# Loads, copies and tile pools at the start and in the last pair, and fewer filler matmuls, in a kernel of attention, soft MoE and feed-forward

## The chip, the cores and the metric

The kernel runs on one core of one Trainium2 chip. The metric is device time in microseconds (us) of one execution, median of three runs. The engines are TensorE (PE in the rows), VectorE (DVE), ScalarE (ACT), GpSimd (POOL) and SyncE (SP, whose queue issues nearly all DMAs); PEld is TensorE's weight load.

## The reference

Three layers follow each other. Attention works on 2 x 8 heads of 768 tokens and 64 values; a query sees only the keys of its own bucket, and a bucket is made of six sign bits:

```python
q_bits = (np.einsum('bhsd,dk->bhsk', q, proj) > 0)      # likewise k_bits
mask = q_bucket[:, :, :, None] == k_bucket[:, :, None, :]
scores = np.where(mask, scale * np.matmul(q, k.transpose(0, 1, 3, 2)), -1000000000.0)
attn = np.exp(scores - np.max(scores, axis=-1, keepdims=True))
attn = attn / (np.sum(attn, axis=-1, keepdims=True) + 1e-09)
x = np.matmul(attn, v)                                   # then (1536, 512)
# soft MoE: 8 experts, 4 slots each
logits = x @ phi
d = softmax over tokens of logits; slot_input = d.T @ x
slot_out[e] = np.maximum(slot_input[e] @ w1[e], 0.0) @ w2[e]
x = softmax over slots of logits @ slot_out
# feed-forward, 512 -> 2048 -> 512
h = x @ w_in
out = (h - np.tanh(h)) @ w_out
```

The inputs are float32, but w_in and w_out come as 64-bit floats and are converted. w1 and w2 are 17 MB each, w_in and w_out 8 MB each.

## The kernel before

The 16 heads are worked on in eight pairs, numbered 0 to 7. Query and key of a pair come as 128 x 768 tiles `xq` and `xk` (64 rows for each head). Matmuls run with rounded fp32 values: `QA` and `KA` hold the rounded part of a head in rows 0 to 63 and the bucket rows and offsets above, `QB` and `KB` hold a copy of the rounded part and the remainder. For each pair the units are: `m`, one tile of maxima (L447 matmul into `pm`, L449 reduce on VectorE into `mx`); `f`, which makes a row of maxima out of them (L454 `mh`, L457 transpose `pc`, L460 and L461, and a small DMA of `row` into `QA`); `s0` and `s1`, scores and exponential for the first and second head (L508 `pst`, L511 on ScalarE into a tile `e`, L521 sum `es` on GpSimd); `a`, product with v (L532 and L536, `pav`); `xr`, `xe`, `x2`, `x3` (sums `pr`, copy `xtu`, scaling and transposed tokens `px`, `xtok`) and `lg`, the MoE logits (L615 `pl`, L618, L624, L625). `wl` and `wc` load and convert w_in.

Pair 0 has units of its own. `const` issues the constants `ct`, `qk` the loads, `hp` and `h` the rounded halves (L379, L381), `b0` the sign bits: L355 writes 4 x 32 partitions of one PSUM tile `pb` (two quarters for the query, two for the key), L361 turns the products into bits in place, and `rows0` (L369 on ScalarE, L371 on VectorE) makes bucket rows of `QA` and `KA` from them. `kc` copies a half of `KA` into `kh1`, `d` copies into `QB` and `KB`, all by DMA (L166). `keep` and `warm` are matmuls into a tile that nobody reads (L718).

The order is written by hand. `START`, `FIRST`, `STEP`, `STEP2` and `LAST` are lists of unit names: START runs first, FIRST in pair 0, STEP to pair 5, STEP2 in pair 6 and LAST in pair 7; units of the next pair are in the list of the one before. `MOE` and `RUN` order the rest. Each engine works in this order of its own instructions, each waiting for its inputs, and SyncE's queue is in order as well.

Tiles come from pools with as many buffers as a number says; a new use waits for the last reader of the old one. `e` tiles come from two pools of NE1 = 12 and NE2 = 7; the second closes within pair 6, so that pairs 6 and 7 have NE1 tiles. Room that a closed pool leaves is opened as a ring of slots for pieces of the expert weights, 1 MB each (`load_pieces`, L249): `RING` gives how many at each place, 21 in all. The third place is in pair 6, when the wide pools close; the fourth and fifth are in pair 7. After the 21st, a piece waits for the release of the slot that it reuses.

`moe` computes dispatch weights `sT`, and then runs the units of MOE: `F` slot inputs (L957), `R`, `T`, `W` and `X` first and second expert product (L970, L934, L981), `H`, `y` (L998) and `z` (L1007) the last experts, `p` and `d` products with w_in (L1036, L1055); `k` is a `keep_clock` of one matmul (two rows in the trace) into `ph`, never read (L805). The last stage, from 300 us, multiplies with w_out in three passes (L1277 to L1279).

Of the kernel before, what the change touches and what calls it, by code (L numbers as in the profile page):

```python
# [68 lines left out]
START = ("const.0 oi.0 qk.0 hp3.0 warm.4 const.1 const.2 b0.0 wl.0 h1.0 h0.0 hp2.0 wk0a.0 wq0v.0 keep.1 wl.0 m.0 wk1a.0 "  # L69
        "kc.0 m.0 m.0 v.0 m.0 m.0 keep.3 l0.0 keep.3 m.0 keep.1 m.0 wq1a.0 m.0 qk.1 keep.1 h2.1 oi.1 h3.1 m.0 keep.3 "  # L70
        "m.0 wl.0 l1.0 m.0 d.0 m.0 v1.0 keep.1 fa.0 m.0 m.0 m.0 v.1 b0.1 l3.0 m.0 m.0 h0.1 m.0 fb.0 h1.1 wl.0 wc.0 "
        "wk1a.1 wq1a.1 s0.0 l2.0 fz.0 wq0a.1 s0.0 v2.0 kc.1 qk.2 s0.0 wk0v.1 keep.1 oi.2 wc.0 s0.0 a.0 wc.0 s0.0 s0.0").split()
FIRST = ("a a a a a a a wc lp fy g0 g1 m l0 l1 wc lp a wl m a vy g2 s0 h1 l2 h3 h0 v qk s1 s0 m s1 m xe d h2 m s0 m m e "
        "wl s1 m xr wl v1 m s1 m m s0 b lg m s0 m s1 s1 m m s0 e s0 s0 m s1 x2 e m e wl lp s1 lp m s1 x3 f2 lp s0 lp wc "
        "s1 s0").split()
# [1336 lines left out]
```

## Time and profile before

| | us |
|---|---|
| median of 3 runs | 455.56 (454.02 to 455.61) |
| the profiled execution | 454.35 |
| its span | 452.6 |
| TensorE busy in the span | 430.2 (95%) |
| VectorE, ScalarE, GpSimd busy | 323.4, 272.5, 285.5 |

The times below are from the profiled execution; its span starts with the first instruction. A row of the windows view gives the stretch, its length, the busy time of each engine with the number of its instructions, the granted TensorE clock (1.00 is full), the mean busy share of the 16 DMA engines, and GB/s. A row of the timeline gives the start, the time from the first to the last of the instructions grouped there, engine, line, operation, output and inputs, shape, count, and, in brackets, the idle time before it and what ended that.

### The profile page before, as it was taken

The numbers are of one execution on the slowest core, as the hardware profiler recorded it, in microseconds if no ns is written. First come the engines' busy times: TensorE is split into PE (matmuls) and PEld (weight loads), VectorE is DVE, ScalarE is ACT, GpSimd is POOL, SyncE is SP. The second block draws the span as 40 slices with busy tenths as digits, with TensorE's granted clock in tenths as the row PEclk, the third lists the DMA queues.
The fourth block names the chain that finished last, engine by engine and source line by source line (L and its number), as shares of the span: only waits on it lengthen the run. The fifth ranks groups of instructions, "written<-read, shape, count | busy, mean of one in ns | idle before, by whom it ended". The sixth has DMA issues, their size and how long they took to land. (4 is left out here: it accounts for less than half of the span.)

```text
span 452.6 us, 7545 instructions
## 1 busy us (share of the span) xinstructions
PE 430.2 (95%) x2621; PEld 298.6 (66%) x2621; DVE 323.4 (71%) x585; ACT 272.5 (60%) x525; POOL 285.5 (63%) x287
## 2 busy tenths in 40 slices
PE   5868999999999999999999998999999999999994
PEld 2446476685858668566767343667777788888883
DVE  4899999999999887484416458299989975454541
ACT  4496658576676947164630111298898978575751
POOL 8759839789797978979660200047788864535350
PEclk9888999999999999999999999999999999999999
DMA  6736454636254543565859999980000003000004
GB/s 197 184 132 168 99 176 135 190 106 187 72 144 159 149 149 117 221 202 234 314 205 421 419 419 420 416 370 0 2 1 2 0 0 141 0 2 0 1 2 146
DMA packets 18166, 71.33 MB, mean 158 GB/s; under 512 B 3492, under 2 KB 4616, under 8 KB 13000
## 3 DMA queue, kind: packets, MB, share of 16 engines
q1 hardware_dynamic: 17976, 70.75, 44.9%
q8 instruction: 23, 0.38, 0.3%
q14 instruction: 23, 0.19, 0.1%
q10 hardware_dynamic: 144, 0.02, 0.0%
HBM read 60.09 MB, written 3.15 MB: 140 GB/s over the span
## 5 line engine op out<-in xcount | busy, mean ns | idle before, releaser
L521 POOL TENSOR_TENSOR es<-es,e 128x512 f32<-128x512 f32 x73 | 92.9, 1286 | 14.4 <-ACT e L511 13.8
L511 ACT ACTIVATE e<-pst 128x512 f32<-128x512 f32 x144 | 77.7, 596 | 40.3 <-PE pst L508 36.1
L449 DVE TENSOR_REDUCE mx<-pm 128x1 f32<-128x512 f32 x144 | 90.2, 677 | 11.7 <-PE pm L447 11.3
L508 PE MATMUL pst<-QA,KA 128*128 128x256 f32 (+1 forms) x192 | 66.7, 362 | 2.1 <-DVE QB L419 1.1
L536 PE MATMUL pav<-e,tv 128*64 128x512 f32 (+1 forms) x384 | 65.0, 489 | 0.0
L508 PE MATMUL pst<-QB,KB 128*128 128x256 f32 (+1 forms) x192 | 63.4, 344 | 0.0
L1227 DVE SCALAR_TENSOR_TENSOR ph<-win,ph 128x512 f32<-128x512 f32 (+1 forms) x64 | 35.7, 558 | 32.6 <-ACT win L1222 31.3
L447 PE MATMUL pm<-KA,QA 96*128 96x512 f32 x192 | 52.7, 361 | 3.6 <-POOL zrw L303 2.9
L1258 POOL TENSOR_TENSOR split<-win,split 128x512 fp32r<-128x512 f32 x31 | 44.9, 1447 | 14.1 <-ACT split L1253 14.1
L1279 PE MATMUL po<-w,split 128*128 128x512 f32 x128 | 51.0, 398 | 0.0
L1277 PE MATMUL po<-w,split 128*128 128x512 f32 x128 | 50.6, 396 | 0.0
L1278 PE MATMUL po<-w,split 128*128 128x512 f32 x128 | 50.4, 394 | 0.0
L536 PEld LDWEIGHTS pav<-e,tv 128*64 128x64 f32 x384 | 26.3, 137 | 33.6 <-issue 27.3
L521 POOL TENSOR_TENSOR es<-e 128x512 f32<-128x512 f32 x30 | 38.9, 1299 | 14.6 <-PE pr L550 9.8
L1258 POOL TENSOR_TENSOR ghl<-win,ghl 128x256 fp32r<-128x256 f32 x32 | 24.2, 756 | 37.0 <-ACT ghl L1253 37.0
L508 PEld LDWEIGHTS pst<-QA,KA 128*128 128x128 f32 x192 | 37.1, 193 | 12.4 <-ACT e L511 4.6
L1222 ACT ACTIVATE win<-ph 128x512 f32<-128x512 f32 (+1 forms) x64 | 30.8, 482 | 22.7 <-PE ph L1215 22.1
L447 PEld LDWEIGHTS pm<-KA,QA 96*128 96x128 f32 x192 | 32.3, 195 | 15.9 <-DVE mx L449 3.9
L1228 DVE SCALAR_TENSOR_TENSOR win<-win,ph 128x512 f32<-128x512 f32 (+1 forms) x64 | 35.5, 555 | 8.3 <-ACT win L1223 0.2
L1223 ACT ACTIVATE win<-win,ct 128x512 f32<-128x512 f32 (+1 forms) x64 | 39.5, 617 | 2.1
L508 PEld LDWEIGHTS pst<-QB,KB 128*128 128x128 f32 x192 | 37.3, 194 | 3.5
L1279 PEld LDWEIGHTS po<-w,split 128*128 128x128 f32 x128 | 24.0, 188 | 7.7 <-POOL split L1258 2.7
(230 smaller groups left out, 803.1 us busy)
## 6 DMA issues: line engine op xcount, KB each, us to landing
...
```

What stands on the lines that cost most here:

```text
L447: nc.tensor.matmul(pm[:, j * 256:j * 256 + c1 - c0], QA[s][h][:96, c * P:(c + 1) * P], KA[s][h][:96, c0:c1], start=True, stop=True)
L449: nc.vector.reduce_max(m, pm.rearrange("p (c k) -> p c k", c=len(cs)), axis=AX.X)
L508: nc.tensor.matmul(pst[:, j * 256:j * 256 + c1 - c0], K[h][:, c * P:(c + 1) * P], Q[h][:, c0:c1], start=x == 0, stop=x == 1)
L511: nc.scalar.activation(e, pst, AF.Exp, scale=0.125)
L521: eng.tensor_tensor(q[0], y, e, ALU.add)
L536: nc.tensor.matmul(pav[i][k][64 * h:64 * h + 64, :], tv[i][:, h, c, :], e2[h][:, j * 256:j * 256 + c1 - c0], start=False, stop=c == KT - 1 ...
L1223: nc.scalar.activation(w, z, AF.Square, bias=ct[:, C_QA:C_QA + 1])
L1227: nc.vector.scalar_tensor_tensor(self.ph[p], z, Q_C, self.ph[p], ALU.mult, ALU.mult)
L1258: (eng or nc.gpsimd).tensor_tensor(gl[p], g, gh[p].bitcast(F32), ALU.subtract)
L1277: nc.tensor.matmul(po, gh[p][:, us], wo.half(f, 0), start=f == 0, stop=False)
L1278: nc.tensor.matmul(po, gh[p][:, us], wo.half(f, 1), start=False, stop=False)
L1279: nc.tensor.matmul(po, gl[p][:, us], wo.half(f, 0), start=False, stop=f == NF - 1)
```

## The change

At the start, `qk.0` goes ahead of the constants, and `b0` of pair 0 is split into `bq` and `bk`, which each take a PSUM tile and compare 64 partitions. The bucket rows of the query are written by ScalarE, those of the first key half by VectorE. The copies `kh1`, `QB` and `KB` of pair 0 are made by ScalarE from `xk` and `xq` (rounded on writing) instead of DMAs from `KA` and `QA`. The `keep` units stand elsewhere, and pair 1's loads come ahead of w_in's. NE1 and NE2 become 10 and 9. `zrw` and `vzw` move from pool `lap` to a pool `zap`, which `head_x` closes; `lap` is closed by itself, before. `RING` gets one slot more in its third place, and the places of pair 7 become 4, 1, 2 and 1 instead of 4, 3 and 2; 21 stay. LAST is ordered anew. In MOE the eight `k.1` are left out.

```diff
-WIDE, NE1, NE2 = 5, 12, 7
+WIDE, NE1, NE2 = 5, 10, 9
-RING, HOLD = (4, 1, 3, 4, 3, 2, 3, 1), 4
+RING, HOLD = (4, 1, 4, 4, 1, 2, 1, 3, 1), 4
-START = ("const.0 oi.0 qk.0 hp3.0 warm.4 const.1 const.2 b0.0 wl.0 h1.0 h0.0 hp2.0 wk0a.0 wq0v.0 keep.1 wl.0 m.0 wk1a.0 "
+START = ("oi.0 qk.0 const.0 hp3.0 const.1 h1.0 warm.4 const.2 bq.0 bk.0 qk.1 wl.0 h0.0 hp2.0 wq0a.0 wk0v.0 keep.1 l0.0 "
...
-LAST = ("a a a a lp xe a s0 s0 lp a a a s0 lp s0 s1 s1 s1 s0 lp xr s0 a a lp x2 x3 s1 s1 lp s1 s0 s0 s0 lp s1 s1 s1 lg "
+LAST = ("a a a s0 lp s0 a a a s0 a lp a s1 xr s0 s0 s1 xe s1 s1 s1 lp s0 lp s1 a a a a lp s0 lp s1 lp x2 s0 lg s1 s0 s1 "
...
-MOE = ("k.1 k.1 k.1 F.0 F.1 R.1 T.0 R.0 W.0 F.2 X.0 W.1 T.2 k.1 T.1 k.1 wm.2 R.2 H.0 F.3 wm.3 X.1 k.1 T.3 W.2 H.1 X.2 "
+MOE = ("F.0 F.1 R.1 T.0 R.0 W.0 F.2 X.0 W.1 T.2 T.1 wm.2 R.2 H.0 F.3 wm.3 X.1 T.3 W.2 H.1 X.2 y.0.1 y.0.0 z.0.0 wm.0 "
...
-        last_x, head_x, early_x, wide_x, xq_x, mid_x, raw_x = (ExitStack() for _ in range(7))
+        last_x, head_x, lap_x, early_x, wide_x, xq_x, mid_x, raw_x = (ExitStack() for _ in range(8))
-        lap = pool("lap", 1, head_x)
+        zap = pool("zap", 1, head_x)
+        lap = pool("lap", 1, lap_x)
-        zrw = lap.tile([P, KT, P], F32R, name="zrw")
-        vzw = lap.tile([P, P], F32R, name="vzw")
+        zrw = zap.tile([P, KT, P], F32R, name="zrw")
+        vzw = zap.tile([P, P], F32R, name="vzw")
...
-        def bits0(i):
-            pb = bt0[i] = psum("pb")
-            halves(i, pb)
-            nc.vector.tensor_scalar(pb[:, :HALF], pb[:, :HALF], 0.0, None, ALU.is_gt)
+        def bits0(i, which):
+            pb = psum("pb")
+            for x in which:
+                bt0[i, x] = pb
+            halves(i, pb, range(2 * which[0], 2 * which[-1] + 2))
+            b = pb[64 * which[0]:64 * which[-1] + 64, :HALF]
+            nc.vector.tensor_scalar(b, b, 0.0, None, ALU.is_gt)
...
-            copy(kh1[i][64:], KA[i % 3][1][:64])
+            nc.scalar.activation(kh1[i][64:], xks[i][64:], AF.Copy)
...
+        def dup(i, which, h):
+            s, t, r0 = i % 3, i % 2, slice(64 * h, 64 * h + 64)
+            if which == 0:
+                nc.scalar.activation(QB[t][h][64:], xqs[i][r0], AF.Copy)
+            else:
+                nc.scalar.activation(KB[t][h][:64], xks[i][r0], AF.Copy)
...
-                if i == last and half.get((i, 0)) == len(SEQ) and len(slots) == sum(RING[:4]) and not xtu and last in pav:
-                    head_x.close()
+                if i == last and len(slots) == sum(RING[:4]) and not xtu and i - 1 not in tv:
+                    lap_x.close()
                     load_pieces(RING[3])
                     open_ring(RING[4], rctx)
                     load_pieces(RING[4])
-                if i == last and half.get((i, 1)) == len(SEQ) and len(slots) == sum(RING[:5]):
-                    last_x.close()
+                if i == last and half.get((i, 0)) == len(SEQ) and len(slots) == sum(RING[:5]) and last in pav:
+                    head_x.close()
                     open_ring(RING[5], rctx)
                     load_pieces(RING[5])
+                if i == last and half.get((i, 1)) == len(SEQ) and len(slots) == sum(RING[:6]):
+                    last_x.close()
+                    open_ring(RING[6], rctx)
+                    load_pieces(RING[6])
```

What this does to the order of instructions is shown at three places. First VectorE at the start, from the first bits to the first `mh`, before:

```order
L361 TENSOR_SCALAR pb<-pb 128x384
L371 TENSOR_SCALAR QA_131<-pb,ct 24x384 x2
L449 TENSOR_REDUCE mx<-pm 128x1 x2
L449 TENSOR_REDUCE mx<-pm 128x2
L449 TENSOR_REDUCE mx<-pm 128x1 x2
L449 TENSOR_REDUCE mx<-pm 128x2
L449 TENSOR_REDUCE mx<-pm 128x1 x2
L449 TENSOR_REDUCE mx<-pm 128x2
L449 TENSOR_REDUCE mx<-pm 128x1 x2
L449 TENSOR_REDUCE mx<-pm 128x2
L454 TENSOR_REDUCE mh<-mx 128x6
```

and the same stretch in the change:

```order
L366 TENSOR_SCALAR pb<-pb 64x384 x2
L376 TENSOR_SCALAR KA_138<-pb,ct 24x384 x2
L461 TENSOR_REDUCE mx<-pm 128x1 x2
L461 TENSOR_REDUCE mx<-pm 128x2
L461 TENSOR_REDUCE mx<-pm 128x1 x2
L461 TENSOR_REDUCE mx<-pm 128x2
L461 TENSOR_REDUCE mx<-pm 128x1 x2
L461 TENSOR_REDUCE mx<-pm 128x2
L461 TENSOR_REDUCE mx<-pm 128x1 x2
L466 TENSOR_REDUCE mh<-mx 128x6
```

The compare is split in two, VectorE writes the key rows and not the query rows, and `mh` stands behind eleven reduces where it stood behind twelve. ScalarE from the first half on, before:

```order
L381 ACTIVATE QA_131<-xq 64x768
L381 ACTIVATE KA_135<-xk 64x768
L369 ACTIVATE KA_135<-pb,ct 24x384 x4
L369 ACTIVATE QA_131<-pb,ct 24x384 x2
L381 ACTIVATE KA_137<-xk 64x768
L381 ACTIVATE QA_133<-xq 64x768
```

and in the change:

```order
L386 ACTIVATE QA_134<-xq 64x768
L386 ACTIVATE KA_138<-xk 64x768
L374 ACTIVATE QA_134<-pb,ct 24x384 x2
L374 ACTIVATE KA_138<-pb,ct 24x384 x2
L394 ACTIVATE kh_199<-xk 64x768
L374 ACTIVATE QA_134<-pb,ct 24x384 x2
L386 ACTIVATE KA_140<-xk 64x768
L386 ACTIVATE QA_136<-xq 64x768
L412 ACTIVATE KB_145<-xk 64x768
L410 ACTIVATE QB_142<-xq 64x768
L412 ACTIVATE KB_145<-xk 64x768
L410 ACTIVATE QB_142<-xq 64x768
```

Query rows of the first head come first, and five copies stand between them and around pair 1's halves. Second, SyncE's queue in pairs 6 and 7 (`w` is a piece of the expert weights, `row` the maxima of pair 7, `rt` and the like small copies), before:

```order
L249 DMA w<-in_moe_w_dram 128x2048
L166 DMA QB_140<-QA_132 64x768
L166 DMA KB_143<-KA_136 64x768
L166 DMA QB_141<-QA_133 64x768
L166 DMA KB_144<-KA_137 64x768
L249 DMA w<-in_moe_w_dram 128x2048 x3
L166 DMA QA_132<-row 1x6x128
L166 DMA QA_133<-row 1x6x128
L166 DMA zrw<-zrow 1x6x128 x4
L249 DMA w<-in_moe_w_dram 128x2048 x13
```

and in the change:

```order
L250 DMA w<-in_moe_w_dram 128x2048
L167 DMA QB_143<-QA_135 64x768
L167 DMA KB_146<-KA_139 64x768
L167 DMA QB_144<-QA_136 64x768
L167 DMA KB_147<-KA_140 64x768
L250 DMA w<-in_moe_w_dram 128x2048 x4
L167 DMA QA_135<-row 1x6x128
L167 DMA QA_136<-row 1x6x128
L167 DMA zrw<-zrow 1x6x128 x4
L250 DMA w<-in_moe_w_dram 128x2048 x12
```

One piece goes from behind the rows to ahead of them. Third, TensorE at the start of MOE, from `sT`'s filler to the product behind T.1, before:

```order
L805 MATMUL po_3069<-ct 128x256
L805 MATMUL ph_3064<-ct 128x256 x3
L957 MATMUL po_3066<-w,sT 32x512 x16
L957 MATMUL po_3067<-w,sT 32x512 x16
L970 MATMUL po_3068<-ct,hold_3187 128x128 x4
L934 MATMUL po_3069<-ct,hold_3188 128x128 x4
L957 MATMUL po_3066<-w,sT 32x512 x16
L981 MATMUL po_3067<-w,hold_3188 32x512 x16
L934 MATMUL po_3068<-ct,hold_3188 128x128 x4
L970 MATMUL po_3069<-ct,hold_3187 128x128 x4
L805 MATMUL ph_3064<-ct 128x256
L970 MATMUL po_3066<-ct,hold_3187 128x128 x4
```

and in the change:

```order
L822 MATMUL po_3077<-ct 128x256
L974 MATMUL po_3074<-w,sT 32x512 x16
L974 MATMUL po_3075<-w,sT 32x512 x16
L987 MATMUL po_3076<-ct,hold_3192 128x128 x4
L951 MATMUL po_3077<-ct,hold_3193 128x128 x4
L974 MATMUL po_3074<-w,sT 32x512 x16
L998 MATMUL po_3075<-w,hold_3193 32x512 x16
L951 MATMUL po_3076<-ct,hold_3193 128x128 x4
L987 MATMUL po_3077<-ct,hold_3192 128x128 x4
L987 MATMUL po_3074<-ct,hold_3192 128x128 x4
```

The three matmuls ahead of the first L957 and the one between the two L970 are gone, and nothing else has moved; one filler stays ahead, into `po`.

## Rows read from the trace of the kernel before

**Rows 1.** Windows: length, busy us (instructions) by engine, clock, DMA share, GB/s.

```profile
20.00:30.00 10.00, 7.34 (x36) 5.19 (x34) 9.06 (x19) 9.05 (x16) 4.84 (x3) 0.83 0.14 42
60.00:200.00 140.00, 139.78 (x928) 95.62 (x928) 123.15 (x228) 92.33 (x176) 118.20 (x118) 1.00 0.51 156
249.30:264.20 14.90, 14.90 (x137) 4.77 (x136) 4.78 (x9) 1.96 (x4) 2.96 (x12) 1.00 1.01 417
```

**Rows 2.** Timeline of all engines at the start, from the first load.

```profile
0.73 0.39 SPq L169 DMA_DIRECT2D ct<-in_const_dram  x1
...
4.13 0.84 ACT L381 ACTIVATE QA<-xq 64x768 fp32r<-64x768 f32 x1 [1.70 <-DMA xq<-in_q_dram]
...
5.62 0.84 ACT L381 ACTIVATE KA<-xk 64x768 fp32r<-64x768 f32 x1 [0.64 <-DMA xk<-in_k_dram]
...
6.53 0.57 DVE L361 TENSOR_SCALAR pb<-pb 128x384 f32<-128x384 f32 x1 [3.55 <-PE pb L355]
...
7.18 1.34 ACT L369 ACTIVATE KA<-pb,ct 24x384 fp32r<-24x384 f32 x2 [0.72 <-DVE pb L361]
...
8.55 1.37 DVE L371 TENSOR_SCALAR QA<-pb,ct 24x384 fp32r<-24x384 f32 x2 [1.46 <-ACT KA L369]
```

**Rows 3.** Timeline of VectorE alone, 9 to 25 us.

```profile
9.96 3.08 DVE L449 TENSOR_REDUCE mx<-pm 128x1 f32<-128x512 f32 x5
14.10 0.69 DVE L449 TENSOR_REDUCE mx<-pm 128x2 f32<-128x512 f32 x1 [1.06 <-PE pm L447]
```

**Rows 4.** Timeline of TensorE, 48 to 49.5 us.

```profile
48.71 0.27 PE L457 MATMUL pc<-ct,mh 128*12 128x128 f32 x1 [1.12 <-DVE mh L454]
```

**Rows 5.** Timeline of SyncE's queue, pairs 6 and 7.

```profile
200.85 1.78 SPq L249 DMA_DIRECT2D w<-in_moe_w_dram  x3
211.05 1.51 SPq L166 DMA_DIRECT2D QA<-row  x2
...
215.59 31.09 SPq L249 DMA_DIRECT2D w<-in_moe_w_dram  x13
```

**Rows 6.** Windows around the last pair and the expert stage.

```profile
202.00:210.00 8.00, 8.00 (x48) 5.20 (x46) 4.20 (x10) 4.18 (x9) 7.84 (x8) 1.00 0.94 387
210.00:216.00 6.00, 6.00 (x45) 4.58 (x44) 2.13 (x5) 2.25 (x5) 5.84 (x6) 1.00 0.02 8
...
228.00:233.00 5.00, 5.00 (x55) 3.27 (x56) 0.56 (x1) 1.09 (x2) 4.08 (x6) 1.00 0.02 7
233.00:268.00 35.00, 33.98 (x300) 18.28 (x300) 15.53 (x37) 4.54 (x9) 4.36 (x16) 1.00 1.01 412
```

**Rows 7.** Timeline of GpSimd in pair 6.

```profile
210.19 1.29 POOL L521 TENSOR_TENSOR es<-e 128x512 f32<-128x512 f32 x1
```

**Rows 8.** Timeline of TensorE in the expert stage.

```profile
247.88 1.46 PE L805 MATMUL ph<-ct 128*128 128x256 f32 x6
249.26 7.07 PE L957 MATMUL po<-w,sT 128*32 128x512 f32 x64
...
265.22 0.60 PE L805 MATMUL ph<-ct 128*128 128x256 f32 x2
265.66 0.60 PE L970 MATMUL po<-ct,hold 128*128 128x128 f32 x4
...
276.75 3.64 PE L981 MATMUL po<-w,hold 128*32 128x512 f32 x32
281.10 1.07 PE L998 MATMUL po<-w,hold 128*32 128x256 f32 x16 [0.70 <-DMA w<-in_moe_w_dram]
...
288.66 1.07 PE L998 MATMUL po<-w,hold 128*32 128x256 f32 x16 [0.31 <-ACT hold L184]
...
291.00 0.68 PE L805 MATMUL ph<-ct 128*128 128x256 f32 x2
```

**Rows 9.** Timeline of VectorE ahead of the expert stage.

```profile
247.56 0.29 DVE L916 TENSOR_TENSOR sT<-po,rden 128x128 f32<-128x128 f32 x1 [0.23 <-PE po L913]
```

**Rows 10.** Timeline of ScalarE near its end.

```profile
287.61 0.39 ACT L1002 ACTIVATE hold<-po 128x256 f32<-128x256 f32 x1 [3.19 <-PE po L998]
```

More of the change, by code (lines that the diff above doesn't have):

```diff
@@ L64 @@
 FORD = [4 * q + 2 * h + i for h in range(2) for q in range(4) for i in range(2)]
-RING, HOLD = (4, 1, 3, 4, 3, 2, 3, 1), 4
-START = ("const.0 oi.0 qk.0 hp3.0 warm.4 const.1 const.2 b0.0 wl.0 h1.0 h0.0 hp2.0 wk0a.0 wq0v.0 keep.1 wl.0 m.0 wk1a.0 "
[L70 to L75, printed above, removed]
+RING, HOLD = (4, 1, 4, 4, 1, 2, 1, 3, 1), 4
+START = ("oi.0 qk.0 const.0 hp3.0 const.1 h1.0 warm.4 const.2 bq.0 bk.0 qk.1 wl.0 h0.0 hp2.0 wq0a.0 wk0v.0 keep.1 l0.0 "
[3 rows of a table added]
+        "s0.0 s0.0 s0.0 keep.1").split()
+FIRST = ("a a a a a a wc a lp fy a g0 g1 m l0 l1 wc lp a wl m vy g2 s0 h1 l2 v qk h3 s1 s0 s1 h0 m xe d h2 m s0 m m wl "
+        "xr s1 m e m m wl v1 s1 m m b lg s0 m s1 m m e s0 m s1 s0 s0 s0 m s1 m x2 lp e wl s1 e lp lp m s1 x3 f2 s0 lp "
+        "s0 wc s1").split()
 STEP = ("d a wc g0 a l0 g1 wc a a l1 h1 fy h0 a a a g2 lp a a l2 h3 vy m wl m s0 s0 m lp m s1 xe m s0 m v m qk e xr b m "
@@ L350, in attention, with halves @@
         bt0 = {}
-        def halves(i, pb):
-            for g in range(4):
+        def halves(i, pb, gs=range(4)):
+            for g in gs:
                 x = (xqs, xks)[g // 2][i]
@@ L366, in rows0 @@
                 rs = slice(32 * (2 * which + j), 32 * (2 * which + j) + 4 * NB)
-                y, b, w = X[i][h][64:64 + 4 * NB, j * HALF:(j + 1) * HALF], bt0[i][rs, :HALF], ct[rs, o:o + 2]
+                y, b, w = X[i][h][64:64 + 4 * NB, j * HALF:(j + 1) * HALF], bt0[i, which][rs, :HALF], ct[rs, o:o + 2]
                 if eng[j % len(eng)] == "a":
@@ L673, in attention @@
             units[f"h{w}"] = lambda i, w=w: his(i, w)
+            units[f"d{'qk'[w % 2]}{w // 2}"] = lambda i, w=w: dup(i, w % 2, w // 2)
             units[f"hv{w}"] = lambda i, w=w: his(i, w, nc.vector)
@@ L718, in unit @@
                     nc.tensor.matmul(wt[0][:32, :w_], wz[:, :32] if w == "warm" else ident[:, :32], wz if w == "warm" else ident, start=True, stop=True)
-            elif w == "b0":
-                bits0(i)
+            elif w in ("b0", "bq", "bk"):
+                bits0(i, {"b0": (0, 1), "bq": (0,), "bk": (1,)}[w])
             elif w[:2] in ("wq", "wk"):
@@ L857, in moe @@
     def moe(mctx, tail, spare, po):
-        open_ring(RING[6], rctx)
+        open_ring(RING[7], rctx)
         mp = mctx.enter_context(tc.tile_pool(name="mp", bufs=1, side="right", reuse_waits="tile"))
-        load_pieces(RING[6])
+        load_pieces(RING[7])
         turns = [2]
@@ L906, in moe @@
         tokx.close()
-        open_ring(RING[7], r3x, "left")
+        open_ring(RING[8], r3x, "left")
         mpl = r3x.enter_context(tc.tile_pool(name="mpl", bufs=1, side="left", reuse_waits="tile"))
-        load_pieces(RING[7])
+        load_pieces(RING[8])
         selpr = mpl.tile([P, C_BLK - C_SELPR], F32, name="selpr")
```

4 lines of the change are left out of this document (2 added, 2 removed), and 9 rows, old and new, of tables (MOE, START).

## The prediction

> **What bounds the kernel now.** I read the stretches first, then the start line by line, then the queue of SyncE around the last pair, then TensorE in the expert stage. [rows 1] splits the run by what each engine did. In 20 to 30 us TensorE works 7.34 of 10 us and VectorE 9.06, so the start hangs on VectorE's maxima. From 60 to 200 us TensorE is busy 139.78 of 140 us: nothing but the number of its instructions counts there, and any lead or delay that it enters with is carried through unchanged. The door between the two is [rows 4]: TensorE stands 1.12 us for VectorE's `mh` and goes on at 48.71 us; that is the last wait of the start. In 210 to 216 and 228 to 233 us TensorE is full too, 6.00 of 6 and 5.00 of 5 [rows 6], so the last pair is TensorE-bound as well. The expert stage is different: from 233 to 268 us the DMA engines are full (1.01, 412 GB/s) [rows 6] while TensorE has a wait of its own only at its end: 0.70 us at 281.10 for an expert piece and 0.31 us at 288.66 [rows 8]. So three places decide: the start up to 48.71, the last pair, and the two chains (pieces, TensorE) that meet at 281.
>
> **The start.** Three things move the first maxima forward.
> (1) The order of loads. The constants are issued at 0.73 us, ahead of xq and xk, and ScalarE starts on xq at 4.13 and on xk at 5.62, both as they land [rows 2]. From xq to xk is 1.49 us for 384 KB, that is 264 KB/us; the constants are 128 x 298 x 4 bytes, 149 KB, so without them ahead xq and xk land 149 / 264 = 0.57 us earlier. The constants now land last of the three, about where xk lands now, which is before the first rows are written; no loss.
> (2) Two banks. Before, bits are compared at 6.53 (0.57 us), ScalarE writes the key rows from 7.18 (1.34 for two), and only then VectorE the query rows, at 8.55 (1.37, after 1.46 idle for ScalarE) [rows 2]. With a bank each, VectorE's key rows and ScalarE's query rows run side by side. TensorE needed both key halves and the first query half, which came at 8.55 + 0.68 = 9.2. In the change both key halves are the last to come: their compare can start 0.57 earlier, at 5.96, ends at 6.53, and the rows end at 6.53 + 1.37 = 7.9. That is 1.3 us with (1) in it. So the first maximum starts not at 9.96 [rows 3] but near 8.65.
> (3) VectorE now does eleven maxima ahead of `mh` where it did twelve, and the fillers stand elsewhere. Its idle of 1.06 us ahead of 14.10, spent on a maximum's matmuls [rows 3], may go. The one maximum less (0.69) only comes later, so I don't count it; of the idle I take half, 0.55. VectorE compares twice now, but the first compare, of the query bits, lies in its idle time before 5.96.
> Five copies go from DMAs to ScalarE, at 0.84 each as the row at 5.62 shows, 4.2 us in all. ScalarE has little queued between 10 and 20 us but pair 1's loads, which come earlier now; the first scores stand behind the second `mh`, so I cost them at nothing; if that cover is gone, it is at most 4.2 us of ScalarE before the first exp, and those are not in VectorE's chain. Three DMA issues leave SyncE, which nobody waits for here.
> Sum: 1.3 + 0.55 = 1.85, say 1.9 us at 48.71. The low end is 1.0 (VectorE's 0.94 us idle in 20 to 30 us eats some of the lead), the high end 1.3 + 1.06 = 2.4.
>
> **The last pair.** Total exp tiles stay 19 for the pairs that use both pools; pairs 6 and 7 have 10 where they had 12. An exp of pair 6 that ScalarE could do near 206.6 then waits for POOL's sum that ends at 211.48 [rows 7]; TensorE has its 20 products with v in that time, so only the bank that this exp holds counts: the second px matmul comes some 0.5 us late. Nearest rows bound the cost: 0 (cover holds) to 0.8; with sums and logits in another order before the end I take 0.35 net.
> The freed tile room takes a ninth expert piece: three pieces were issued from 200.85, four are now; thirteen from 215.59, twelve are now [rows 5]. Before, the DMA engines rested from 210 to 216 us (0.02 busy) and from 228 to 233 [rows 6]. Thus 1 MB goes into a hole and leaves the full stretch that starts at 233: 1.049 MB / 412 GB/s = 2.5 us off that chain. Its price is on SyncE's queue: the row of pair 7 is issued at 211.05 [rows 5], and at 387 GB/s [rows 6] four pieces from 200.85 need about 11 us, until 212.6, so the row lands near 214.5, while its first reader comes at about 215. I take nothing, with 1 us as the upper bound. The Trainium skill (DMA: Bandwidth & Descriptors, Queues, rings and completion order) says that each DMA engine consumes descriptors in ring order; by that the row can't pass the piece, which is the bound just taken, and no run here shows it yet.
>
> **The expert stage.** Two chains have to be shortened together. TensorE's: eight filler units go. A pair of filler matmuls costs 0.44 us (265.22 to 265.66 [rows 8], start to start). Three units ahead of F.0 go: its input `sT` was ready at 247.56 + 0.29 = 247.85 [rows 9], and the six matmuls at 247.88 held TensorE until 249.26, so 3 x 0.44 = 1.3 of that. Two around T.1 give 0.88, one behind X.1 0.44: 2.6 in all before 281. One near 283.7 lies under ScalarE's copy, and of the one at 291.00 (0.44) I take 0.15, since `soT` is awaited right behind it; the bounds are 0 and 0.44. Before, TensorE ended X.2 at 280.39 (276.75 + 3.64) and waited to 281.10, a slack of 0.7. So the fillers alone would give nothing at 281.10, and the piece alone no more than 0.7; only together they move it.
> TensorE's end of X.2: 280.39 - 2.6 + 0.35 = 278.1. The piece: 281.10 - 2.5 - 0.3 (its chain starts 0.3 earlier, its first release, pair 6's part of the logits, coming sooner in the order) = 278.3. So y.0.1 starts at 278.3, 2.8 earlier. The matmuls at 288.66 wait for the last piece, I judge: the profile puts the wait down to ScalarE's L184, but their own input was copied at 287.61 + 0.39 = 288.0 [rows 10], and 288.66 is three pieces of 2.5 us behind 281.1. So they move by 2.8 too. With 0.15 more this is 2.95, say 3.0 us at the hand-over to the last stage, which is TensorE work in a row.
>
> **Sum.** 454.35 - 1.9 - 3.0 = 449.45 for the profiled execution; the median of the runs, 455.56, is 1.0027 times that, so **450.7 us**.
>
> **Rivals.**
> *(A) The start gains, the expert stage doesn't.* It would be so if slots, not transfers, pace the pieces: piece after piece waits for a release by TensorE, or the row of pair 7 stalls TensorE by the whole 1 us and the exps by 0.8. For: the pieces are issued in groups of one to three, behind releases. Against: DMA is full throughout 233 to 268. 454.35 - 1.9 + 0.3 = 452.75, thus 454.0.
> *(B) The start's lead is lost before 48.71,* because VectorE is the bound in 20 to 48 us and gets no instruction less. For: 9.06 of 10 busy. Against: what it has to do after is the same, so an earlier start should be an earlier end. 454.35 - 3.0, thus 452.6.
> *(C) Slower: TensorE's clock falls when the fillers are gone.* Place: F.0 and F.1, 64 matmuls in 7.07 us from 249.26 [rows 8]. At 1.2 instead of 2.4 GHz they take 7.07 more; TensorE's chain then ends X.2 at 278.1 + 7.1 = 285.2, 4.1 later than before, and less 1.9 and 0.15 the whole is 2.05 longer: 456.4, thus 457.6; with the next such stretch, to 264.2, at half clock too it is up to 7 more, and I put C at 460. It decides from 5.1 us of loss (what the rest gives is 4.85, and 0.2 lies in TensorE's slack). For: the fillers compute nothing that is read, and the six at 247.88 stand right ahead of F.0. Against: F.0's input is there at 247.85, so no gap opens; and from 249.3 to 264.2, without a filler, TensorE was busy 14.90 of 14.90 us at a granted clock of 1.00, the full level [rows 1].
> The Trainium skill (TensorE: Matmul & The Clock Gate, Part 1: The HAM clock gate) says that the idle array is throttled to 1.2 GHz and activity releases it. By that rule the change is a risk wherever it opens a gap; its price is that of (C), and the row without fillers agrees that work alone holds the clock.
>
> **How the numbers follow.** Forecast 0.65, A 0.17, B 0.11, C 0.07. The ends of the forecast: start 1.0 to 2.4, expert stage 2.0 (row stall of 1 us) to 3.3 (no stall anywhere), so 448.65 to 451.35, thus 449.9 to 452.6; the runs shown spread by 1.6 us, so 0.8 less below. The range has to take in B and most of A: 449.0 to 454.0, and leaves out C and a tenth beside it. About 0.5%, 2.3 us, is what a measurement of this kernel can tell from no change, so faster means below 453.3: forecast 0.65, B 0.11 and a part of A, 0.05; same is the rest of A, 0.12; slower is C.
>
> **What would show it.** The first maximum of VectorE near 8.65 and the last `mh` of the start handed over at 46.8 instead of 48.71; TensorE from there at full work. DMA busy in 210 to 213, and the row of pair 7 with no TensorE wait behind it. The expert stage with 1.00 clock, F.0 within 0.3 us of `sT`, y.0.1 some 4.7 us before 281.1 (start and stage together), with a wait for a piece of under 0.5 us. I am wrong if `mh` is handed over after 47.7, if a wait of over 1 us stands on TensorE between 200 and 233, or if a slice after 240 has a clock under 0.9.

## The result: 450.25 us, and the profile after

The changed kernel takes 450.25 us (median of four runs, 448.8 to 450.9) against 455.0 (four runs of the kernel before, 454.02 to 455.61): a ratio of 0.9878, with a 95% interval of 0.9843 to 0.9913. 450.7 was predicted, with 449.0 to 454.0. The profiled execution took 448.8 us, its span 447.0 (452.6 before). One run further down, of no_fill_cut (456.77 us at a granted clock of 0.94), fell in the chip's slower state and is left out of that kernel's median and spread.

The start, timeline of all engines, with the names as ahead of the prediction; these rows answer to [rows 2, 3]:

```profile
4.15 0.84 ACT L386 ACTIVATE QA<-xq 64x768 fp32r<-64x768 f32 x1 [1.72 <-DMA xq<-in_q_dram]
...
5.18 0.84 ACT L386 ACTIVATE KA<-xk 64x768 fp32r<-64x768 f32 x1 [0.18 <-DMA xk<-in_k_dram]
...
5.46 1.21 DVE L366 TENSOR_SCALAR pb<-pb 64x384 f32<-64x384 f32 x2 [2.48 <-PE pb L357]
...
6.05 1.35 ACT L374 ACTIVATE QA<-pb,ct 24x384 fp32r<-24x384 f32 x2
...
6.76 1.38 DVE L376 TENSOR_SCALAR KA<-pb,ct 24x384 fp32r<-24x384 f32 x2
...
8.29 0.70 PE L459 MATMUL pm<-KA,QA 96*128 96x512 f32 x2 [2.25 <-DVE KA L376]
```

ScalarE's query rows (6.05) and VectorE's key rows (6.76) now overlap, and the first maximum starts 1.08 us earlier on TensorE (9.37 before). VectorE then does the eleven maxima ahead of its first `mh` without a pause, and hands over the last `mh` of the start at 45.42 where [rows 4] has 48.71 (VectorE and TensorE, timelines of each):

```profile
8.79 6.90 DVE L461 TENSOR_REDUCE mx<-pm 128x1 f32<-128x512 f32 x11 [0.66 <-PE pm L459]
```

```profile
45.42 0.28 PE L469 MATMUL pc<-ct,mh 128*12 128x128 f32 x1 [1.02 <-DVE mh L466]
```

SyncE's queue in pairs 6 and 7, which answers to [rows 5], and TensorE from the last pair on, which answers to [rows 8]:

```profile
190.14 9.35 SPq L250 DMA_DIRECT2D w<-in_moe_w_dram  x4
207.46 1.52 SPq L167 DMA_DIRECT2D QA<-row  x2
...
213.25 30.44 SPq L250 DMA_DIRECT2D w<-in_moe_w_dram  x12
```

```profile
208.54 0.44 PE L613 MATMUL px<-ct,xtu 128*128 128x128 f32 x2 [0.34 <-ACT e L523]
...
244.99 7.07 PE L974 MATMUL po<-w,sT 128*32 128x512 f32 x64
...
271.13 3.64 PE L998 MATMUL po<-w,hold 128*32 128x512 f32 x32
275.03 1.07 PE L1015 MATMUL po<-w,hold 128*32 128x256 f32 x16 [0.26 <-DMA w<-in_moe_w_dram]
276.65 1.07 PE L1015 MATMUL po<-w,hold 128*32 128x256 f32 x16 [0.54 <-ACT hold L1019]
278.22 0.63 PE L1024 MATMUL po<-selpr,hold 128*128 128x32 f32 x4 [0.50 <-ACT hold L1019]
...
280.34 1.28 PE L1015 MATMUL po<-w,hold 128*32 128x256 f32 x16
281.39 1.95 PE L1053 MATMUL po<-win,lg 128*32 128x256 f32 x16
283.09 1.73 PE L1015 MATMUL po<-w,hold 128*32 128x256 f32 x16
```

F.0 starts at 244.99 (249.26 before), y.0.1 at 275.03 (281.10 before), 6.07 earlier, with a wait of 0.26 for a piece where it was 0.70. Up to here each time is as forecast or earlier. But sixteen matmuls with `lg`, 1.05 us elsewhere, take 1.95 at 281.39, and those at 283.09 take 1.73 and not 1.07. The windows view gives the reason (the column behind the five engines is the granted clock):

```profile
281.00:282.00 1.00, 1.00 (x16) 0.55 (x12) 0.28 (x1) 0.26 (x1) 0.00 (x0) 0.53 1.05 434
...
283.00:284.00 1.00, 1.00 (x16) 0.47 (x12) 0.00 (x0) 0.00 (x0) 0.00 (x0) 0.50 1.00 401
```

TensorE's clock was at its lower level, 0.50 (1.2 of 2.4 GHz), from 281.1 to 284.5 us, a stretch that has 1.00 in the kernel before. The last stage starts at 295.46 instead of 300.53, so of the 6.07 us 5.07 are left, and 5.03 at the last matmul.

### The profile page after: what moved, and what is told of

It reads as the page before. It is cut to its first block, busy times and chain, and to the rows that moved or that the text cites. A ratio compares the mean times of both kernels' runs of the same rounds, so it can differ in the third digit from the quotient of the medians.

```text
span 447.0 us, 7512 instructions
## 1 busy us (share of the span) xinstructions
PE 426.6 (95%) x2605; PEld 294.5 (66%) x2605; DVE 323.8 (72%) x586; ACT 276.3 (62%) x530; POOL 285.8 (64%) x287
## 5 line engine op out<-in xcount | busy, mean ns | idle before, releaser
L1239 ACT ACTIVATE win<-ph 128x512 f32<-128x512 f32 (+1 forms) x64 | 30.8, 481 | 22.9 <-PE ph L1232 22.2
L459 PEld LDWEIGHTS pm<-KA,QA 96*128 96x128 f32 x192 | 31.3, 189 | 16.1 <-DVE mx L461 5.3
```

The source lines that it names most:

```text
L459: nc.tensor.matmul(pm[:, j * 256:j * 256 + c1 - c0], QA[s][h][:96, c * P:(c + 1) * P], KA[s][h][:96, c0:c1], start=True, stop=True)
```

## The experiments

To compare executions, each profile is cut at three points: the row of maxima ahead of the pairs (the row of [rows 4]), the one of pair 7, and the start of y.0.1. The times from pair 7's row on turn out to repeat to 0.2 us between executions with the same code from there on and the same clock; the times up to it don't. All in us; "fall" says where, between y.0.1 and the last stage, a clock under 1.00 was seen. The last column is of all the runs of a kernel, the others are of one profiled execution. The ratios in the text are to the kernel before, run beside each group: 455.0, 455.54, 455.79 and 455.60 us.

| kernel | first maximum | row before the pairs | row of pair 7 | from it to F.0 | to y.0.1 | y.0.1 to last stage | pair 7's row to last matmul | fall | median of runs |
|---|---|---|---|---|---|---|---|---|---|
| before | 9.37 | 48.71 | 210.12 | 39.14 | 70.98 | 19.43 | 236.70 | none | 455.56 |
| changed | 8.29 | 45.42 | 206.53 | 38.46 | 68.50 | 20.43 | 235.26 | 281 | 450.25 |
| start_only | 8.92 | 47.57 | 208.70 | 39.15 | 70.94 | 19.38 | 236.75 | none | 454.09 |
| fill_only | 9.80 | 50.14 | 211.47 | 37.91 | 70.94 | 22.98 | 240.23 | 283 to 293 | 460.76 |
| room_only | 9.59 | 50.37 | 211.75 | 39.75 | 70.69 | 18.96 | 235.93 | none | 455.25 |
| room_fill | 9.34 | 50.00 | 211.28 | 38.46 | 68.54 | 20.35 | 235.16 | 285 | 454.04 |
| no_fill_cut | 8.43 | 48.40 | 209.53 | 39.75 | 70.70 | 18.96 | 235.91 | none | 449.82 |
| after_again | 8.92 | 48.90 | 210.06 | 38.46 | 68.58 | 20.69 | 235.10 | 296 | 451.78 |
| two_gaps | 8.92 | 47.58 | 208.68 | 38.47 | 68.53 | 19.19 | 233.93 | none | 450.22 |
| two_gaps_b | 8.35 | 48.31 | 209.41 | 38.45 | 68.44 | 19.20 | 233.93 | none | 451.10 |
| one_bank | 10.08 | 49.92 | 211.03 | 38.46 | 68.54 | 19.19 | 234.01 | none | 453.86 |
| const_first | 8.98 | 48.92 | 210.03 | 38.46 | 68.59 | 19.18 | 234.10 | none | 451.80 |
| warm_gaps | 8.92 | 46.44 | 207.62 | 38.45 | 68.64 | 19.18 | 234.08 | none | 448.76 |

Four kernels ran first, on one chip.

**start_only**: the changed start, with pools, rings, LAST and MOE of before. Against the changed kernel:

```diff
-WIDE, NE1, NE2 = 5, 10, 9
+WIDE, NE1, NE2 = 5, 12, 7
-RING, HOLD = (4, 1, 4, 4, 1, 2, 1, 3, 1), 4
+RING, HOLD = (4, 1, 3, 4, 3, 2, 3, 1), 4
... (zap and lap_x taken back, LAST and MOE as before)
```

> The changed start alone: order of loads, two banks, copies by ScalarE, the lists START and FIRST; pools, rings, LAST and MOE as before. The changed kernel's trace has the last mh of the start handed over at 45.42 instead of 48.71 us. Theory (the lead is carried through the stretch in which TensorE is full): hand-over at 45.4, F.0 of the expert stage at 249.26 - 3.4 = 245.9, y.0.1 at 277.7, and the total 3.4 us below the kernel before, ratio 0.9925. Rival (the lead runs into the pieces' transfers or into a wait for GpSimd or ScalarE in the pairs and is lost in part): total 1 to 2 us below, ratio 0.996 to 0.998, with a new wait on TensorE between 50 and 240 us or a longer wait for a piece at y.0.1.

454.09 us, ratio 0.9959 (0.9937 to 0.9982): 1.9 us by the ratio, less than the 3.4 and as the rival had it. But the rival's new wait isn't there, and this kernel's own row before the pairs came at 47.57, not 45.42, with the same instructions up to there. Cut at that row, the theory holds: pair 7's row follows 161.13 us later (161.11 in the changed kernel, 161.41 before), and y.0.1 has a wait of 0.66, as before. No lead is lost on the way; the lead itself differs by execution, which the later experiments take up.

**fill_only**: the kernel before with MOE of the change.

```diff
-MOE = ("k.1 k.1 k.1 F.0 F.1 R.1 T.0 R.0 W.0 F.2 X.0 W.1 T.2 k.1 T.1 k.1 wm.2 R.2 H.0 F.3 wm.3 X.1 k.1 T.3 W.2 H.1 X.2 "
+MOE = ("F.0 F.1 R.1 T.0 R.0 W.0 F.2 X.0 W.1 T.2 T.1 wm.2 R.2 H.0 F.3 wm.3 X.1 T.3 W.2 H.1 X.2 y.0.1 y.0.0 z.0.0 wm.0 "
... (all eight k.1 left out)
```

> The kernel before without the eight filler units of MOE and nothing else. Theory (two chains meet at y.0.1): X.2 ends 2.6 us earlier, at 277.8, but y.0.1 still starts at 281.1, with a wait of about 3.3 us for a piece; total the same as before within 0.5 us, or up to 1.5 us longer if that wait makes the granted clock fall to half behind it, as it did at 281 to 284.6 us in the changed kernel. Rival (the fillers alone set the stage): y.0.1 at 278.5, total 2.6 us shorter.

460.76 us, ratio 1.0102 (1.0069 to 1.0135): slower, by more than the theory had put at its far end. TensorE and the windows view:

```profile
282.41 1.42 PE L1009 MATMUL po<-w,hold 128*32 128x256 f32 x16 [3.17 <-DMA w<-in_moe_w_dram]
284.36 1.94 PE L1009 MATMUL po<-w,hold 128*32 128x256 f32 x16 [0.53 <-ACT hold L1013]
...
290.78 1.94 PE L1009 MATMUL po<-w,hold 128*32 128x256 f32 x16
```

```profile
285.00:290.00 5.00, 4.50 (x30) 3.40 (x20) 0.16 (x1) 0.57 (x3) 0.00 (x0) 0.50 1.01 419
290.00:295.00 5.00, 5.00 (x60) 2.75 (x60) 0.76 (x2) 1.13 (x3) 0.00 (x0) 0.68 1.01 415
```

F.0 comes 1.23 us earlier and X.2 another 1.3, and y.0.1 starts not a bit earlier: 70.94 us behind pair 7's row. The 2.5 us gained turn into a wait of 3.17 for the piece, and behind that wait the clock is at 0.50 from 283 to 293 us, so the way from y.0.1 to the last stage takes 3.55 us more. Of the 4.9 us by which the last matmul is later than before, 1.35 stand already at pair 7's row, ahead of anything that was edited. The rival is out: alone, leaving the fillers out is a loss.

**room_fill**: the changed kernel with START, FIRST and the copy of `kh1` as before.

```diff
-            nc.scalar.activation(kh1[i][64:], xks[i][64:], AF.Copy)
+            copy(kh1[i][64:], KA[i % 3][1][:64])
... (START and FIRST as before)
```

> Tile room, rings, LAST and the missing fillers together, with the start as before. Theory: y.0.1 at 281.10 - 2.6 = 278.5 (a piece earlier and fillers gone, less 0.5 lost in the last pair), a wait for a piece of under 0.5 us there; behind it a stretch at half clock takes 1.0 us back; total 1.6 to 2.2 us below the kernel before, ratio 0.9955. Rival (the gain at y.0.1 in the changed kernel came with the earlier start): total within 0.5 us of before.

454.04 us, 0.9966 (0.9939 to 0.9993): 1.5 us by the ratio, a little under the theory's 1.6 to 2.2. y.0.1 starts 68.54 us behind pair 7's row, 2.44 earlier than before, as in the changed kernel (68.50), with a wait of 0.30. So this gain has nothing to do with the start. And 0.9 us is given back behind it, with a clock of 0.50 for some us from 285 on.

**two_gaps**: the changed kernel with two filler units, in the waits at y.0.0 and z.0.0. The second stood there before too; the first is at a place where the kernel before had none.

```diff
-H.1 X.2 y.0.1 y.0.0 z.0.0 wm.0
+H.1 X.2 y.0.1 k.1 y.0.0 k.1 z.0.0 wm.0
... (the rest of MOE as it is)
```

> The changed kernel with two filler units put back, one in each of the two waits for ScalarE behind y.0.1 and y.0.0 (0.54 and 0.50 us, a unit takes 0.44). Theory (TensorE's waits between 274.8 and 278.2 us brought the clock to half from 281.0 to 284.6, and that cost the 1.0 us between y.0.1, 6.07 earlier than before, and the last stage, 5.04 earlier): clock 1.00 in every stretch from 270 to 300, the last stage starts at 294.5 instead of 295.46, total 1.0 us below the changed kernel, about 449.2. Rival 1 (the loss is from elsewhere, such as the last piece): clock 1.00, last stage at 295.4, total as the changed kernel. Rival 2 (two units are too little): clock at half again, total as the changed kernel.

The profile's stage does as the theory has it: clock 1.00 from 270 to 297 us, 19.19 us from y.0.1 to the last stage, 1.24 less than the changed kernel. The total of 450.22 us doesn't show it; in the profiled execution the row before the pairs came at 47.58, 2.16 later than the changed kernel's. So four more ran, on one chip again, with the changed kernel among them.

**after_again**: the changed kernel itself.

> The changed kernel once more, to be compared with the next one on the same chip. Theory: 450.2 us, ratio 0.988; the granted clock is at half again for some us behind y.0.0 and y.1.0 (20.4 us from y.0.1 to the last stage, where before takes 19.4). Rival: the clock falls there in some executions only, and this one shows 19.2 to 19.4 us.

451.78 us, 0.9906 (0.9879 to 0.9933). Neither of the two: from y.0.1 on the clock stayed at 1.00 up to 296 us and was 0.57 from 296 to 300, where eight filler matmuls that both kernels keep ran just ahead of the last stage (TensorE):

```profile
296.17 3.68 PE L822 MATMUL po<-ct 128*128 128x256 f32 x8
```

They take 1.99 us in two_gaps_b. So the loss is of the same size, 1.5 us against two_gaps, at another place. Of the five profiles with the changed kernel's MOE and tile room (changed, room_fill, after_again, one_bank, const_first) three have such a fall and two have none.

**two_gaps_b**: as two_gaps.

> The changed kernel with two filler units in the waits behind y.0.1 and y.0.0, again, beside the changed kernel. Its first profile had clock 1.00 all through the expert stage and 19.19 us from y.0.1 to the last stage, 1.24 less than the changed kernel. Theory (that is a saving in every execution): median 1.2 us below the changed kernel's, ratio 0.985 to 0.986. Rival (the fall of the clock comes in few executions of the changed kernel, or start and stage trade places): medians within 0.4 us of each other.

451.10 us, 0.7 below the changed kernel beside it, less than the 1.2 of the theory; the two ratios' intervals overlap (0.9868 to 0.9915 here). In the profile the stage repeats to 0.01 us, 19.20 us. The clock of 1.00 is seen in each of three profiles with the two units, and in two of five without; the two without a fall take 19.18 and 19.19 us as well, so the units save nothing where the clock holds anyway. As a difference of medians the saving is not resolved by these runs.

The mean granted clock, on record for every run, bears on it. With the new start, all 33 runs that keep two or all eight units (start_only, two_gaps, two_gaps_b, warm_gaps and the five of no_fill_cut) have 0.984 or more. Of the 27 with none of them (changed, after_again, one_bank, const_first) eleven have 0.973 to 0.979, and these are the slowest runs of their kernels. In which stretch their clock was low isn't on record, and one_bank and const_first differ at the start too; so this speaks for the units and doesn't show by itself where they act.

**no_fill_cut**: the changed kernel with MOE as before, all eight fillers.

```diff
-MOE = ("F.0 F.1 R.1 T.0 R.0 W.0 F.2 X.0 W.1 T.2 T.1 wm.2 R.2 H.0 F.3 wm.3 X.1 T.3 W.2 H.1 X.2 y.0.1 y.0.0 z.0.0 wm.0 "
+MOE = ("k.1 k.1 k.1 F.0 F.1 R.1 T.0 R.0 W.0 F.2 X.0 W.1 T.2 k.1 T.1 k.1 wm.2 R.2 H.0 F.3 wm.3 X.1 k.1 T.3 W.2 H.1 X.2 "
... (as before)
```

> The changed kernel with the eight filler units of MOE back as before, so new start and new tile room alone. From the first runs, the parts count from the last row of maxima (pc of pair 7): to F.0 39.14 us before, 0.55 more with the new room, 1.23 less without fillers; from F.0 to the end of X.2 31.13 before, 1.3 less without fillers. Theory (two chains): here 39.7 and 31.13, so y.0.1 comes 70.9 us behind that row, with no wait for a piece, where before came 70.98; the piece alone gives 0.1, the clock stays 1.00, and the total is that of the new start, ratio 0.995 to 0.996. Rival (the piece was what counted): y.0.1 68.5 behind that row, ratio 0.990.

The stage is as expected: F.0 39.75, y.0.1 70.70 behind pair 7's row, with no wait for a piece (TensorE):

```profile
276.77 3.64 PE L998 MATMUL po<-w,hold 128*32 128x512 f32 x32
280.23 1.05 PE L1015 MATMUL po<-w,hold 128*32 128x256 f32 x16
```

The total, 449.82 us and 0.9881 (0.9846 to 0.9917), is not: the theory wanted a ratio of 0.995 to 0.996. Its five runs go from 449.46 to 453.23. The profiled one, 452.39, is among the upper two. If the stage took as long in all five, the three at 449.5 to 449.8 had pair 7's row near 206.6 to 207.0 (an estimate: their times less the 242.86 us that the profiled one has behind its row), as in the changed kernel's first profile. So the totals don't tell whether all fillers or none is better; the stage does, for a given start: 235.91 us from pair 7's row to the last matmul with all, 235.1 to 235.3 with none and a fall, 234.0 to 234.1 with none and no fall, 233.93 with two.

**room_only**: the kernel before with pools, rings and LAST of the change.

```diff
-WIDE, NE1, NE2 = 5, 12, 7
+WIDE, NE1, NE2 = 5, 10, 9
-RING, HOLD = (4, 1, 3, 4, 3, 2, 3, 1), 4
+RING, HOLD = (4, 1, 4, 4, 1, 2, 1, 3, 1), 4
... (zap, lap_x and LAST of the change)
```

> Tile room, rings and LAST alone, with the start and the fillers of before. Theory (two chains): F.0 39.7 us and y.0.1 70.9 us behind the last row of maxima (39.14 and 70.98 before), no wait for a piece at y.0.1, total the same as before within 0.5 us. Rival 1 (the piece counts alone): 2 to 2.5 us below before. Rival 2 (fewer exp tiles cost more than 0.55): over 0.5 us above.

455.25 us, 0.9987 (0.9968 to 1.0006), the same as before. F.0 39.75 us and y.0.1 70.69 behind pair 7's row: the price of the last pair is 0.61 at F.0, more than the 0.35 taken, and the piece gives the 0.7 of the old wait and no more at y.0.1. The last piece comes earlier too, which the theory had left out: 18.96 us from y.0.1 to the last stage, 0.47 less than before. Fillers gone and the piece moved are worth 2.4 us together, and 0.0 and 0.3 alone.

Three more asked what the start is made of.

**one_bank**: the changed kernel with the bits of pair 0 in one PSUM tile.

```diff
-const.2 bq.0 bk.0 qk.1
+const.2 b0.0 qk.1
... (the rest of START as it is)
```

> The changed kernel with the query and key bits of pair 0 in one PSUM tile again, compared in one instruction; ScalarE still writes the query rows, VectorE the key rows. The changed kernel's first maximum matmul started at 8.29 to 8.92 us in seven profiles. Theory (the second bank lets both engines write rows at once and saves one row pair): VectorE's key rows start behind ScalarE's query rows, 1.3 us later, first maximum matmul at 9.6 to 10.2 us. Rival (the two engines share the tile without waiting, and the order of loads alone moved the start): first maximum matmul within 0.3 us of 8.3 to 8.9.

453.86 us, 0.9952 (0.9926 to 0.9978). VectorE waits 1.48 us for ScalarE again, as in [rows 2] with the parts exchanged, and the first maximum starts at 10.08 (VectorE, then TensorE):

```profile
6.51 0.57 DVE L366 TENSOR_SCALAR pb<-pb 128x384 f32<-128x384 f32 x1 [3.53 <-PE warm L731]
8.55 1.38 DVE L376 TENSOR_SCALAR KA<-pb,ct 24x384 fp32r<-24x384 f32 x2 [1.48 <-ACT QA L374]
```

```profile
10.08 1.19 PE L459 MATMUL pm<-KA,QA 96*128 96x512 f32 x2 [3.57 <-DVE KA L376]
```

That is 1.2 to 1.8 us behind the 8.29 to 8.92 of the two tiles, and the rival, no wait, is out. The Trainium skill (PSUM — Partial Sum Buffer, PSUM bank collisions raise a hardware error) says that two engines may use one bank at once in different quarters of the partitions, and the query and key rows lie in different quarters; so it is the program's wait on the tile that costs this, not the memory.

**const_first**: the changed kernel with the constants ahead of xq and xk.

```diff
-START = ("oi.0 qk.0 const.0 hp3.0 const.1
+START = ("const.0 oi.0 qk.0 hp3.0 const.1
... (the rest of START as it is)
```

> The changed kernel with the constants loaded ahead of xq and xk again, nothing else. Seven profiles of the new order have ScalarE starting on xq at 3.91 to 4.15 and on xk at 4.91 to 5.18; with the constants first it was 4.13 to 4.25 and 5.59 to 5.66. Theory (the prediction's 0.57 us, of which the profiles show 0.5 to 0.7 on xk and only 0.1 on xq): xk at 5.6, first maximum matmul 0.45 later, at 8.8 to 9.3. Rival (xk isn't what the key bits wait for, since TensorE has them late in any case): first maximum matmul still at 8.3 to 8.9.

451.80 us, 0.9935 (0.9908 to 0.9962), the same as the changed kernel within the intervals. xq is used at 4.21 and xk at 5.87, so the constants hold up xk by 0.7 to 1.0 us and xq by at most 0.4. The first maximum is at 8.98, inside the theory's 8.8 to 9.3, though only 0.06 behind the later of the new order's starts. Those starts come in two kinds, by how TensorE's bit matmuls run in the execution: they take some 0.85 us each at first and 0.49 to 0.51 from a moment on that varies, which fits a clock at its lower level up to there. The trace's record of the granted clock begins, with 1.00, at 4.6 to 5.0 us in the three profiles with a first maximum at 8.29 to 8.43, and at 6.1 us or later in those with 8.92. In const_first it begins at 5.2. So against its like the order of loads is worth some 0.6 us at that point, and against the other kind 0.1.

**warm_gaps**: two_gaps with six filler matmuls and not one in TensorE's idle time ahead of the first maximum.

```diff
-wq0a.0 wk0v.0 keep.1 l0.0
+wq0a.0 wk0v.0 keep.6 l0.0
... (the rest of START as it is, MOE as in two_gaps)
```

> The kernel with two filler units behind y.0.1 and y.0.0, and in the start six filler matmuls instead of one ahead of the first maximum, where TensorE stands idle for 2.3 to 2.5 us. The profiles of the new start fall in two kinds: one had a granted clock of 1.00 from 7.5 to 20 us and the row of maxima before the pairs at 45.42, the others 0.50 between 10 and 12.5 us and that row at 47.6 to 48.9, their fillers ahead of maxima (eight for 1.91 us instead of 1.06) standing on VectorE's way. Theory (the idle ahead of the first maximum costs the clock, and the clock costs 2 to 3 us): clock 1.00 from 7.5 to 20 us, that row at 45.4 to 45.8, total about 448.5, ratio 0.984. Rival 1 (the clock falls whatever stands there): 0.50 between 10 and 15 us, row at 47.5 or later, total as with the two units alone, 450.2 to 451.1. Rival 2 (the six fillers run at half clock themselves and delay the first maximum): first maximum matmul after 9.2 us, total up to 0.5 above that.

448.76 us, 0.9839 (0.9814 to 0.9863): below the changed kernel and two_gaps, and its five runs lie within 1.4 us, from 447.71 to 449.12. Both rivals are out in its profile: the clock is 1.00 from 7.5 to 20 us, and the first maximum starts at 8.92. This is what the start's clock does. In after_again, windows, VectorE and TensorE:

```profile
10.00:12.50 2.50, 2.50 (x9) 1.93 (x9) 2.26 (x5) 2.42 (x5) 2.44 (x5) 0.50 0.99 368
12.50:15.00 2.50, 2.50 (x11) 1.46 (x10) 1.56 (x3) 2.48 (x4) 0.52 (x2) 0.50 0.55 220
```

```profile
14.38 0.69 DVE L461 TENSOR_REDUCE mx<-pm 128x1 f32<-128x512 f32 x1 [0.94 <-PE pm L459]
16.77 2.58 DVE L461 TENSOR_REDUCE mx<-pm 128x1 f32<-128x512 f32 x4 [1.70 <-PE pm L459]
```

```profile
14.27 1.91 PE L731 MATMUL warm<-ct 128*32 128x128 f32 x8
```

and in warm_gaps:

```profile
10.00:12.50 2.50, 2.50 (x16) 1.85 (x17) 2.50 (x6) 2.42 (x5) 2.44 (x5) 1.00 1.02 370
12.50:15.00 2.50, 2.50 (x20) 1.90 (x17) 2.46 (x6) 2.48 (x4) 0.36 (x1) 1.00 0.59 236
```

```profile
9.43 6.90 DVE L461 TENSOR_REDUCE mx<-pm 128x1 f32<-128x512 f32 x11 [0.65 <-PE pm L459]
```

```profile
12.21 1.06 PE L731 MATMUL warm<-ct 128*32 128x128 f32 x8
```

At 0.50 TensorE is busy all 2.50 us and yet late: the matmuls and the fillers between them take nearly twice as long, and VectorE waits 0.94 and 1.70 us for maxima that it takes in one run of 6.90 us when the clock is 1.00. The row before the pairs is at 46.44, against 47.6 to 48.9 in the profiles with 0.50; the theory had 45.4 to 45.8. Of the 1.02 us behind the changed kernel's first profile, 0.63 come from the first maximum, at 8.92 and not 8.29; the rest arises later, where the clock was at 0.50 from 23.9 to 30.8 us and not from 21.7 to 25.1 only. That first profile happened to have the clock at 1.00 up to 21.7 us without help. One profile shows the effect of the six; the mean granted clocks of the five runs, 0.989 to 0.995 where after_again has 0.977 to 0.988, agree with it.

## Why the prediction was right, point by point

**The start** was put at 1.9 us, in a range of 1.0 to 2.4. The two first profiles show 3.29 at the row before the pairs. That is a lucky pair, and by the prediction's own limit, wrong if `mh` is handed over after 47.7, three of six executions would have failed it: the six profiles of the unaltered new start have this row at 45.42, 48.40, 47.57, 47.58, 48.31 and 48.90 (mean 47.70), the four of the old at 48.71, 50.14, 50.00 and 50.37 (mean 49.81). The means differ by 2.1 us, near the forecast, while a single execution can be off by 2. Inside, the terms were shared out wrongly. Loads: xk came 0.4 to 1.0 us earlier (5.59 to 5.84 before, 4.86 to 5.18 after), where 0.57 was taken, xq by less (4.13 to 4.27 before, 3.80 to 4.15 after), so the constants did not hold up both by their size. Two banks: 0.7 us taken, 1.2 to 1.8 measured by one_bank. VectorE's idle: half of 1.06 taken; in the first profile all of it went, in after_again 2.88 us stand between the first maximum and `mh`, and the clock decides. The prediction read the 1.06 us as matmuls of a maximum and did not ask at which clock these ran; [rows 1] has 0.83 from 20 to 30 us, and the same question at 10 to 15 us was not put. The trace of the kernel before answers it: TensorE was busy all the time, at 0.68 and 0.64, and ahead of that maximum's matmuls, which begin at 13.26, stood twelve fillers (windows, then TensorE):

```profile
10.00:12.50 2.50, 2.50 (x15) 1.84 (x14) 2.50 (x5) 2.46 (x4) 2.44 (x5) 0.68 1.01 266
12.50:15.00 2.50, 2.50 (x10) 1.32 (x8) 1.25 (x3) 0.16 (x1) 2.42 (x3) 0.64 1.03 370
```

```profile
10.70 2.63 PE L718 MATMUL warm<-ct 128*32 128x128 f32 x12
13.26 0.80 PE L447 MATMUL pm<-KA,QA 96*128 96x256 f32 x2
```

ScalarE's five copies cost nothing, as said: it had done them by 16.84 us in the profile, 5 us ahead of the first scores (22.18).

**Carried through** was right: from the row before the pairs to pair 7's row it is 161.28 to 161.41 us with the old lists and 161.10 to 161.16 with the new, in every profile of the table that has one or the other unaltered. Rival B is out.

**The last pair** was put at 0.35; room_only and no_fill_cut show 0.61 at F.0. 0.34 is the px matmul that waits for ScalarE's exp, the mechanism named with 0.5. The row of pair 7 stalled nothing: SyncE issued the four pieces from 190.14 to 199.5, earlier than the 200.85 that the prediction reckoned with, and TensorE has no wait for the row. (From 200.85 the prediction's own numbers, four pieces at 387 GB/s, give 211.7 and not 212.6; nothing hung on it.) The piece went into another hole than was said: one that the kernel before has 8 to 10 us ahead of its row (0.13 busy from 200 to 202 us). In the changed kernel the DMA engines were full up to the row, and the rest behind it, where the prediction wanted them busy, stayed (windows):

```profile
200.00:206.50 6.50, 6.50 (x37) 3.77 (x35) 2.76 (x5) 2.77 (x6) 6.34 (x7) 1.00 1.00 417
206.50:213.00 6.50, 6.16 (x45) 4.59 (x44) 2.23 (x5) 1.74 (x4) 6.34 (x7) 1.00 0.15 60
```

**The expert stage up to y.0.1** was put at 2.8 with both chains moved, and at 0 and up to 0.7 with one. From pair 7's row it is 2.4 to 2.5 with both, 0.04 with the fillers alone and 0.29 with the piece alone. 2.5 + 0.3 was taken for the piece; the 0.3, for a chain that starts earlier, did not come: the pieces of the full stretch are issued from 22.0 us behind pair 7's row in both kernels (from 232.09 before, 228.54 after). This reading, two chains with 0.7 us between them, is the step that the runs bear out best. Rival A is out.

**Behind y.0.1** is where the prediction failed, and by its own sign: a slice after 240 with a clock under 0.9 (0.85 from 279.4 to 290.5 us in the first profile). It costed the fillers there at a gain of 0.15 us; the way to the last stage got 0.9 to 1.3 us longer in three of five profiles and 0.25 shorter in two (19.18 and 19.19 us against 19.43), where the tile room alone makes it 0.47 shorter. Rival C had the mechanism, the clock at its lower level once fillers are gone, but put it at F.0, where no gap opens and where the clock stayed 1.00 in every profile, with a price of 7 us. It came where TensorE waits three times in a row (0.26, 0.54 and 0.50 us at 275.03, 276.65 and 278.22), and behind the one wait of 3.17 us in fill_only. The Trainium skill (TensorE: Matmul & The Clock Gate, Part 1: The HAM clock gate) says that the array's clock is throttled unless activity releases it. The trace agrees where the wait is long, at 0.50 behind the 3.17 us of fill_only. For short waits the rows leave it open: the kernel before has 0.70 and 0.54 us there and no fall, with one filler unit in the third wait's place (TensorE, before):

```profile
282.71 1.07 PE L998 MATMUL po<-w,hold 128*32 128x256 f32 x16 [0.54 <-ACT hold L1002]
283.71 0.70 PE L805 MATMUL ph<-ct 128*128 128x256 f32 x2
```

So only this one of the eight stood beside the waits at which the clock is lost. That the three waits bring the fall is the likeliest reading of the profiles with and without units in them, three of three at 1.00 against two of five, and is not shown beyond that.

**The sum** came out within 0.5 us of the median in part by luck, since the errors offset each other: the first runs' start gave more than forecast, the expert stage gave less (1.44 us from pair 7's row to the last matmul, where 2.95 was forecast), and the second set of runs of the same kernel, 451.78 us, still lies in the range.

What stays open: why one execution has the clock at 1.00 at the start and another not, with the same program, and whether the spread of the unprofiled runs (2.3 us for the changed kernel in its second set, 3.8 for no_fill_cut) is all from there. That warm_gaps with its clock held spreads by 1.4 us speaks for it, and doesn't show it.
